# The last pass of a two-layer attention and MLP backward: row vectors prepared one set ahead on two partition pairs, and fourteen weight-gradient pieces moved into the first group

## The chip, the cores and the metric

The kernel runs on one core of a Trainium2 chip. The time is the device time of one execution in microseconds; three runs of the kernel before gave 1993.6, 1994.94 and 1997.81 us, median 1994.94 us. The engines are named as in the profile: PE is the matrix engine, PEld its weight loads, DVE, ACT and POOL are the vector, scalar and GpSimd engines, and SP only issues DMAs. DMAs that are issued from SP, ACT and POOL show up as the DMA queues q1, q10 and q0.

## The reference

One token goes through attention A, MLP B, A and B again with the same weights, and then back:

```
x = x + A(layernorm(x))      # layer 1:  q = x@wq, softmax(q k^T) v over 65536 cached keys, @wo
x = x + B(layernorm(x))      # layer 2:  relu(x@w1 + b1)^2 @ w2 + b2
x = x + A(layernorm(x))      # layer 3
x = x + B(layernorm(x))      # layer 4
grads = vjp(grad_out)        # of x, k_cache, v_cache, wq, wo, w1, b1, w2, b2
```

All data are bf16. `k_cache` and `v_cache` are 4 heads x 65536 x 128 (67 MB each), D is 1024, there are 32 query heads (8 to a cached head), F is 3584, `wq` is 1024 x 4096, `wo` 4096 x 1024, `w1` 1024 x 3584, `w2` 3584 x 1024. Each weight gradient is a sum of two outer products of vectors, one from each layer that uses the weight: for `w2`, for example, g4 gx^T + g2 dx2^T. So a weight gradient takes hardly any arithmetic, but each has to be written in full (7.3 to 8.4 MB).

## The kernel before, in words

The kernel goes over the cached keys and values four times: forward of layer 1, forward of layer 3, backward of layer 3, and a last pass (`attn_bwd4`) that does the backward of layer 1 and writes the gradients of the keys and values for both layers. The change is in this last pass, which starts at about 1217 us of the span.

The last pass takes the four cached heads ("groups") in the order 3, 2, 1, 0, and each group in 64 steps of 8 columns (8 x 128 keys). `pipeline` runs 256 + 7 iterations; in each it issues three stages, `vT` (8 transposes of V, L1015), `vS` two steps later (products with dO, L1035; every fourth step the tile X, whose halves come from DVE, L1042 and L1043, and from POOL, L1044 and L1045, and its transposes, L1050) and `k8` seven steps behind `vT` (dq, L1072; the gradients of 8 columns of K and V, L1082). The gradients leave PSUM by `evac` (L152 on ACT, L155 on DVE; whichever has less planned load) into one of three staging pairs, and after every fourth step POOL issues two stores of 1 MB (L1089, L1090). K and V come in slabs of 1 MB that SP issues (L278) into a ring of five areas as these come free; the second group's end adds two areas.

Beside the three stages an iteration can have background work, `bg[i]`, issued at its end and pinned behind what each engine has been given (`in_order`). There are two kinds. The first is the row dots: `og1.later` reads 8 rows of `wo` (256 KB each, 2 KB to a partition, L809) for each of the groups 2, 1 and 0, and `qg1.early` and `qg1.transposed` read rows of `wq` (L864); a row dot is a multiplication on DVE (L427) and a sum on ACT (L428). The second is the weight gradients, planned from iteration 73 (one after the end of the first group) to 244: 154 tasks, spread evenly. Of these 38 are pieces of `rows_into`: they turn four columns of two vectors into 512 elements in partitions 0 and 1 of `long_rows` or `short_rows` (two casts on DVE, L1103; four matmuls with two columns of weights, L1106; one evacuation of 2 x 512). The other 116 are units of `outer2`: two matmuls of 512 columns (L1133) with 128 partitions, all but two of them zero, an evacuation of 128 x 1024 (or less), and after every second unit a store of 512 KB (384 KB for some of `out_6`), issued by POOL (L1137). There is one set of rows at a time: the pieces for the next weight stand between the units of the one before and its own. The order is `out_8` (w2), `out_6` (w1), `out_4` (wq) for groups 3 and 2, `out_5` (wo), `out_4` for group 1. Group 0 of `out_4` follows behind the pipeline. The stores have five staging areas of 512 KB, four of them in the exponentials of the first group, which are free once this group is done.

`long_rows` is `area[12]` and `short_rows` a quarter of `area[13]`; both are set to zero by POOL (L1354, L1355). Of the eight `wo` rows of the second group, each has a buffer of its own, and SP issues them 30 iterations ahead.

Of the kernel before, what the change touches and what calls it, by code (L numbers as in the profile page):

```python
# [8 lines left out]
BF = mybir.dt.bfloat16  # L9
# [5 lines left out]
P = 128  # L15
# [3 lines left out]
def kernel(  # L19
# [52 lines left out]
    OG = 2048  # L72
# [1023 lines left out]

    def rows_into(rows, cols, nj):

        def piece(j0):
            jn = min(4, nj - j0)  # L1100
            cc = tmp.tile([P, 4, 2], BF, name="r2_cc")
            for l in range(2):
                nc.vector.tensor_copy(out=cc[:, 0:jn, l], in_=cols[l][:, j0:j0 + jn])  # L1103
            pt = ps_gg()
            for jj in range(jn):
                nc.tensor.matmul(pt[0:2, jj * P:(jj + 1) * P], lhsT=cc[:, jj, :], rhs=ident_b[:, :], start=True, stop=True)  # L1106
            evac(rows[0:2, j0 * P:(j0 + jn) * P], pt[0:2, 0:jn * P], kind="f32")
        for j0 in range(0, nj, 4):
            yield lambda j0=j0: piece(j0)

    def outer2(stages, out_dram, a_rows, K, b_rows, c0, N):
# [3 lines left out]
        av = a_rows[:, 0:K].rearrange("q (p k) -> q k p", k=KB)  # L1115
# [7 lines left out]
        for kb, per, n0, w in pieces:  # L1123
            for kk in range(per):
                for m0 in range(0, w, 1024):
                    def unit(kb=kb, per=per, n0=n0, w=w, kk=kk, m0=m0):
# [193 lines left out]
    ring.add(area[7], area[12])  # L1320
# [16 lines left out]
    ring.remove(area[7], area[12])  # L1337
# [4 lines left out]

    PS["pool"].release()
# [3 lines left out]
    long_rows, short_rows = area[12], part(area[13], 0, 1024)  # L1347
    wo_rows = Turn([part(area[13], i, 1024) for i in (1, 2)] + [part(area[5], 1, 1024)])
    e_first = [e_tiles[k][ORD4[0]] for k in (1, 3)]
# [3 lines left out]
    def rows_ready():  # L1353
        nc.gpsimd.memset(long_rows, 0.0)  # L1354
        nc.gpsimd.memset(short_rows, 0.0)  # L1355

    def gwq_tasks(gs, fresh=True):
        gs = sorted(gs)
        a, b = gs[0] * R, (gs[-1] + 1) * R
        if fresh:  # L1360
            yield from rows_into(short_rows, [L3["n"][:], L1["n"][:]], DC)
        yield from rows_into(long_rows, [dqT3[:, a:b], dqT1[:, a:b]], b - a)
        yield from outer2(stages, out_4, short_rows, D, long_rows, gs[0] * GD, len(gs) * GD)

    def gw_tasks():
        yield from rows_into(short_rows, [gx[:], dx2[:]], DC)
        yield from rows_into(long_rows, [L4["g"][:], L2["g"][:]], FC)
        yield from outer2(stages, out_8, long_rows, F, short_rows, 0, D)
        yield from rows_into(short_rows, [L4["n"][:], L2["n"][:]], DC)
        yield from rows_into(long_rows, [dh4[:], dh2[:]], FC)  # L1370
        yield from outer2(stages, out_6, short_rows, D, long_rows, 0, F)
        yield from gwq_tasks(ORD4[0:2])
        yield from rows_into(short_rows, [dx3[:], dx1[:]], DC)
        yield from rows_into(long_rows, [L3["oT"][:], L1["oT"][:]], HQ)
        yield from outer2(stages, out_5, long_rows, QD, short_rows, 0, D)
        yield from gwq_tasks(ORD4[2:3])
# [3 lines left out]
    first_rows = Turn(wo_rows.areas + [part(area[12], i, 1024) for i in range(4)])  # L1380
    og1.later(vbx1, ORD4[1], bg, 16, 5, first_rows, 30, nc.sync)
# [14 lines left out]
    def group_done(j):  # L1396
        if j == 1:
# [14 lines left out]
    for t in gwq_tasks(ORD4[-1:], False):  # L1412
        t()
# [32 lines left out]
```

## Time and profile before

| what | us |
|---|---|
| median of three runs | 1994.94 |
| profiled execution: device time | 1996.7 |
| profiled execution: span from first to last instruction | 1994.9 |
| busy PE, PEld, DVE, ACT, POOL | 1590.6, 1316.1, 1101.0, 1026.5, 204.4 |
| mean rate of the DMA engines over the span | 398 GB/s |
| mean granted clock of the matrix engine | 0.903 |

Times in the tables of stretches are microseconds from the start of the span. "DMA share" is the mean busy share of the core's 16 DMA engines; 1.0 means that all were busy all the time (overlapping packets let it read 1.01 or 1.02). A group of instructions is given with the idle time of its engine just before it and what ended that idle time. Idle time of an engine that is not the bottleneck costs nothing.

### The profile page before, as it was taken

To read this page: it belongs to the slowest core of one execution; us is meant where nothing else is said; L and a number is where in the kernel's file an instruction comes from. 1 tells how busy PE (TensorE), PEld (TensorE's weight loads), DVE (VectorE), ACT (ScalarE), POOL (GpSimd) and SP (SyncE) were. 2 spreads that over 40 slices of the span, in tenths; PEclk is the share of its full clock that TensorE was granted. 3 is DMA by queue.
4 is the path that set the end of the run, shared out by engine and by line. 5 is a ranking of instruction groups with operands and counts; after the bars stand their busy time and mean duration, and the time that the engine had idled before them with its cause. 6 is when DMAs were issued, how large, how long until landed. Compare 5 with 4: busy or idle time off the path is not lost.

```text
span 1994.9 us, 65729 instructions
## 1 busy us (share of the span) xinstructions
PE 1590.6 (80%) x29868; PEld 1316.1 (66%) x29924; DVE 1101.0 (55%) x1816; ACT 1026.5 (51%) x1284; POOL 204.4 (10%) x362
## 2 busy tenths in 40 slices
PE   7888886579888858888878876877888778788886
PEld 6878786578787757877777775555555545555464
DVE  4544431146444314645454456877677767787675
ACT  3543432034434314445444436876677667767775
POOL 0000000000000000000000001222122222212221
PEclk9998997669999976999889977999889978989898
DMA  9999999989999996999999996999999999999997
GB/s 395 426 423 421 411 408 410 406 317 419 425 421 420 425 409 275 397 418 412 412 412 396 403 390 240 412 425 424 387 418 408 423 406 367 423 372 420 423 422 302
DMA packets 119186, 793.86 MB, mean 398 GB/s; under 512 B 11756, under 2 KB 11770, under 8 KB 55290
## 3 DMA queue, kind: packets, MB, share of 16 engines
q1 hardware_dynamic: 82858, 604.02, 74.1%
q0 software_dynamic: 29136, 173.04, 21.0%
q10 hardware_dynamic: 6912, 12.59, 1.7%
q8 instruction: 234, 3.83, 0.8%
q14 instruction: 46, 0.38, 0.0%
HBM read 623.92 MB, written 165.69 MB: 396 GB/s over the span
## 4 chain that ended last, share of the span: by engine, by line
PE 38%; DMA 34%; DVE 10%; ACT 10%; issue 7%; another core or an unknown queue 0%; POOL 0%; SPq 0%; ACTq 0%; POOLq 0%; DVEq 0%
DMA pair<-in_A_v_cache_dram 15%; DMA pair<-in_A_k_cache_dram 8%; DMA out_dram<-pair 7%; PE ps_tr L667 6%; PE ps_sc L686 4%; PE ps_acc L729 4%; PE ps_gg L1082 4%; PE ps_tr L920 3%; PE ps_tr L1015 3%; ACT small L152 3%; ACT pair L152 3%; DVE pair L155 3%; DMA pair<-in_A_wo_dram 2%; DVE small L155 2%; PE ps_sc L941 2%
## 5 line engine op out<-in xcount | busy, mean ns | idle before, releaser
L155 DVE COPY small<-ps_tr 128x1024 bf16<-128x1024 bf16 x637 | 432.2, 688 | 338.1 <-PE ps_tr L667 172.8
L152 ACT COPY small<-ps_tr 128x1024 bf16<-128x1024 bf16 x371 | 372.8, 1015 | 387.6 <-PE ps_tr L667 206.8
L152 ACT CAST pair<-ps_gg 128x1024 bf16<-128x1024 f32 (+2 forms) x331 | 320.3, 983 | 141.1 <-PE ps_gg L1082 79.0
L155 DVE CAST pair<-ps_gg 128x1024 bf16<-128x1024 f32 x245 | 289.4, 1182 | 115.5 <-PE ps_gg L1082 91.3
L667 PE MATMUL ps_tr<-ident_b,pair 128*128 128x128 bf16 x3264 | 246.8, 225 | 29.2 <-DMA pair<-in_A_k_cache_dram 16.4
L1082 PE MATMUL ps_gg<-pair,small 64*128 64x512 bf16 x1024 | 201.5, 403 | 56.1 <-ACT pair L152 24.1
L667 PEld LDWEIGHTS <-pair 128*128 128x128 bf16 x3264 | 197.4, 101 | 34.8 <-DMA pair<-in_A_k_cache_dram 19.0
L729 PE MATMUL ps_acc<-eT,pair 128*128 128x64 bf16 x3840 | 170.4, 205 | 44.6 <-DMA pair<-in_A_v_cache_dram 39.8
L686 PE MATMUL ps_sc<-L_qpad,small 128*128 128x64 bf16 (+7 forms) x3456 | 173.9, 193 | 24.0 <-issue 10.7
L729 PEld LDWEIGHTS <-pair 128*128 128x128 bf16 x3840 | 154.0, 104 | 48.3 <-DMA pair<-in_A_v_cache_dram 42.9
L1015 PE MATMUL ps_tr<-ident_b,pair 128*128 128x128 bf16 x1792 | 163.4, 229 | 14.8 <-DMA pair<-in_A_v_cache_dram 11.6
L428 ACT ACTIVATE pair<-pair 128x1024 bf16<-128x1024 bf16 (+1 forms) x125 | 142.1, 1137 | 50.3 <-DVE pair L427 46.1
L920 PE MATMUL ps_tr<-ident_b,pair 128*128 128x128 bf16 x2048 | 155.6, 228 | 13.6 <-DMA pair<-in_A_v_cache_dram 9.8
L686 PEld LDWEIGHTS <-small 128*128 128x128 bf16 x3456 | 140.4, 99 | 34.6 <-ACT small L152 16.1
L1015 PEld LDWEIGHTS <-pair 128*128 128x128 bf16 x1792 | 115.7, 102 | 61.3 <-issue 42.8
L920 PEld LDWEIGHTS <-pair 128*128 128x128 bf16 x2048 | 128.6, 103 | 35.7 <-DMA pair<-in_A_v_cache_dram 17.8
L1082 PEld LDWEIGHTS <-small 64*128 64x128 bf16 x1024 | 60.5, 94 | 112.5 <-issue 85.0
L941 PE MATMUL ps_sc<-B_dOpad,small 128*128 128x64 bf16 (+7 forms) x2048 | 101.0, 193 | 16.0 <-ACT small L152 9.0
L1035 PE MATMUL ps_sc<-DOB,small 128*128 128x64 bf16 (+3 forms) x2048 | 112.1, 195 | 0.6 <-issue 0.2
L1035 PEld LDWEIGHTS <-small 128*128 128x128 bf16 x2048 | 87.0, 100 | 36.9 <-issue 32.0
L692 DVE TENSOR_REDUCE pm_all<-pair 128x8 f32<-128x512 f32 x64 | 43.9, 686 | 111.8 <-ACT pair L691 111.8
L941 PEld LDWEIGHTS <-small 128*128 128x128 bf16 x2048 | 80.1, 99 | 26.1 <-ACT small L152 14.1
(262 smaller groups left out, 1997.0 us busy)
## 6 DMA issues: line engine op xcount, KB each, us to landing
out_dram<-pair POOLq DMA_DIRECT2D x128, 1024.0 KB, 16.3
pair<-in_A_v_cache_dram SPq DMA_DIRECT2D x62, 2048.0 KB, 16.9
pair<-in_A_v_cache_dram SPq DMA_DIRECT2D x112, 1024.0 KB, 13.0
pair<-in_A_k_cache_dram SPq DMA_DIRECT2D x111, 1024.0 KB, 13.9
pair<-in_A_k_cache_dram SPq DMA_DIRECT2D x55, 2048.0 KB, 19.0
pair<-in_A_wo_dram SPq DMA_DIRECT2D x24, 1024.0 KB, 19.4
out_dram<-eT POOLq DMA_DIRECT2D x44, 512.0 KB, 16.5
pair<-in_B_w_dram SPq DMA_DIRECT2D x24, 896.0 KB, 15.1
```

The lines of the kernel that those rows point to most:

```text
L152: nc.scalar.copy(out=out, in_=in_)
L155: nc.vector.tensor_copy(out=out, in_=in_)
L428: nc.scalar.activation(out=view, in_=view, func=ACTF.Copy, accum_out=ycol)
L667: nc.tensor.transpose(pt[:, i, :], kb8[:, i, :], ident_b[:, :])
L686: nc.tensor.matmul(ps_s[:, slot:slot + w, :].rearrange("p a b -> p (a b)"), lhsT=kt[:, i, :], rhs=L["qpad"][:, g, 0:w, :].rearrange("p a b ...
L692: nc.vector.tensor_reduce(out=pm_all[:, :, c0 // UB], in_=S_sb[:, :, c0:c0 + un], axis=AX.X, op=ALU.max)
L729: nc.tensor.matmul(ps_o[:, :, :].rearrange("p a b -> p (a b)"), lhsT=vb8[:, i, :], rhs=eT[g][:, :, c:c + 8], start=(c == 0), stop=(c == C ...
L920: nc.tensor.transpose(pt[:, i, :], vb8[:, i, :], ident_b[:, :])
L941: nc.tensor.matmul(ps_dp[:, slot:slot + w, :].rearrange("p a b -> p (a b)"), lhsT=vt[:, i, :], rhs=dOpad[:, g, 0:w, :].rearrange("p a b -> ...
L1015: nc.tensor.transpose(pt[:, i, :], vb8[:, i, :], ident_b[:, :])
L1035: nc.tensor.matmul(ps_dp[:, slot:slot + w, :].rearrange("p a b -> p (a b)"), lhsT=vt[:, i, :], rhs=DOB[:, g, 0:w, :].rearrange("p a b -> p ...
L1082: nc.tensor.matmul(pg[:, t2 * 512:(t2 + 1) * 512], lhsT=xt[64 * t2:64 * t2 + 64, blk0 + half, :], rhs=GG[64 * t2:64 * t2 + 64, :, :, :].re ...
```

## The change

Rows are now made by `rows_moved`: the columns of both vectors are laid side by side (two casts), transposed once on PE, copied by DVE to `flat`, and two DMAs issued by POOL put the `nj` pieces of 256 bytes of each vector behind each other into one partition. A set of rows lies in partitions 0 and 1, or in 64 and 65; `outer2` takes the 64 partitions from `at_row` on, so one set can be made while the other is in use. `rows_into` is left for the last group only.

The first 14 units (of 28) of `out_8` move into the first group, two in an iteration, at iterations 3, 11, ... 51; until the first group is done there is a single staging area for them. The other 102 tasks are spread from iteration 73 to 244. The order of the weights becomes `out_8`, `out_6`, `out_5`, `out_4`.

`long_rows` is set to zero before the slabs of `w1` are read, so the ring borrows `area[13]` in place of `area[12]` there; `short_rows` is set to zero, and the first set of rows made, just before the last pass. The eight `wo` rows of the second group are now issued by ACT, 8 iterations ahead, into the three buffers of `wo_rows`.

```
+    def rows_moved(rows, cols, nj, flat=None):
+        cc = tmp.tile([P, 64], BF, name="rm_cc")
+        for l in range(2):
+            nc.vector.tensor_copy(out=cc[:, l * nj:(l + 1) * nj], in_=cols[l])
+        pt = ps_tr()
+        nc.tensor.transpose(pt[0:2 * nj, 0, :], cc[:, 0:2 * nj], ident_b[:, :])
+        if flat is None:
+            flat = tmp.tile([64, P], BF, name="rm_flat")
+        nc.vector.tensor_copy(out=flat[0:2 * nj, :], in_=pt[0:2 * nj, 0, :])
+        for l in range(2):
+            nc.gpsimd.dma_start(out=rows[l:l + 1, 0:nj * P], in_=flat[l * nj:(l + 1) * nj, :])
...
-    def outer2(stages, out_dram, a_rows, K, b_rows, c0, N):
+    def outer2(stages, out_dram, a_rows, K, b_rows, c0, N, at_row):
...
-        av = a_rows[:, 0:K].rearrange("q (p k) -> q k p", k=KB)
+        rows = slice(at_row, at_row + 64)
+        av = a_rows[rows, 0:K].rearrange("q (p k) -> q k p", k=KB)
...
-                                             rhs=b_rows[:, n0 + m0 + q0:n0 + m0 + q0 + qq], start=True, stop=True)
+                                             rhs=b_rows[rows, n0 + m0 + q0:n0 + m0 + q0 + qq], start=True, stop=True, tile_position=(at_row, 0))
...
-    ring.add(area[7], area[12])
+    long_rows, short_rows = area[12], part(area[13], 0, 1024)
+    nc.gpsimd.memset(long_rows, 0.0)
+    ring.add(area[7], area[13])
...
+    nc.gpsimd.memset(short_rows, 0.0)
+
+    def rows_a():
+        rows_moved(short_rows[64:66, :], [gx[:], dx2[:]], DC, area[13][0:64, 1024:1024 + P])
+        rows_moved(long_rows[64:66, :], [L4["g"][:], L2["g"][:]], FC, area[13][0:64, 1024 + P:1024 + 2 * P])
...
+    rows_a()
...
-    stages = Turn([part(e, i, OG) for i in range(2) for e in e_first] + [area[5][:, SLOT - OG:SLOT]])
+    stages = Turn([area[5][:, SLOT - OG:SLOT]])
...
-    first_rows = Turn(wo_rows.areas + [part(area[12], i, 1024) for i in range(4)])
-    og1.later(vbx1, ORD4[1], bg, 16, 5, first_rows, 30, nc.sync)
+    og1.later(vbx1, ORD4[1], bg, 14, 5, wo_rows, 8, nc.scalar)
...
-    at(bg, done[0], rows_ready)
-    i0, i1 = done[0] + 1, IPG * G - 12
-    tasks = list(gw_tasks())
-    for t, fn in enumerate(tasks):
-        at(bg, i0 + t * (i1 - i0) // len(tasks), fn)
+    tasks = list(outer2(stages, out_8, long_rows, F, short_rows, 0, D, 64))
+    na = len(tasks)
+    tasks += list(outer2(stages, out_6, short_rows, D, long_rows, 0, F, 0))
+    nb_ = len(tasks)
+    tasks += list(outer2(stages, out_5, long_rows, QD, short_rows, 0, D, 64))
+    tasks += outer_q(ORD4[0:2], 0) + outer_q(ORD4[2:3], 2 * GD)
+    n0, i0, i1 = 14, done[0] + 1, IPG * G - 12
+    place = [3 + 8 * (t // 2) for t in range(n0)] + [i0 + t * (i1 - i0) // (len(tasks) - n0) for t in range(len(tasks) - n0)]
+    for i, fn in zip(place, tasks):
+        at(bg, i, fn)
+    at(bg, 20, rows_b)
+    at(bg, place[na - 1] + 1, rows_c)
+    at(bg, place[nb_ - 1] + 1, rows_d)
+    at(bg, max(place[nb_ - 1], done[1]) + 2, lambda: rows_q(ORD4[0:2], 0))
+    at(bg, done[2] + 2, lambda: rows_q(ORD4[2:3], 2 * GD))
...
     def group_done(j):
-        if j == 1:
+        if j == 0:
+            stages.areas += [part(e_tiles[k][ORD4[0]], i, OG) for i in range(2) for k in (1, 3)]
+        elif j == 1:
             ring.add(e_area(1, ORD4[1]), e_area(3, ORD4[1]))
```

More of the change, by code (lines that the diff above doesn't have):

```diff
@@ L1336 @@
     og1.first(ORD4[0], dx1, vbx1)
-    ring.remove(area[7], area[12])
+    ring.remove(area[7], area[13])
     gb2 = add_cols(gx[:], dx2[:], "gb2")
@@ L1341, with rows_b, rows_c, rows_d @@
     col_to_dram(gb1, F, out_7, nc.gpsimd)
+    nc.gpsimd.memset(short_rows, 0.0)
+    def rows_a():
+        rows_moved(short_rows[64:66, :], [gx[:], dx2[:]], DC, area[13][0:64, 1024:1024 + P])
+        rows_moved(long_rows[64:66, :], [L4["g"][:], L2["g"][:]], FC, area[13][0:64, 1024 + P:1024 + 2 * P])
+    def rows_b():
+        rows_moved(short_rows[0:2, :], [L4["n"][:], L2["n"][:]], DC)
+        rows_moved(long_rows[0:2, :], [dh4[:], dh2[:]], FC)
+    def rows_c():
+        rows_moved(short_rows[64:66, :], [dx3[:], dx1[:]], DC)
+        rows_moved(long_rows[64:66, :], [L3["oT"][:], L1["oT"][:]], HQ)
+    def rows_d():
+        rows_moved(short_rows[0:2, :], [L3["n"][:], L1["n"][:]], DC)
+    def rows_q(gs, at_):
+        sl = slice(min(gs) * R, (max(gs) + 1) * R)
+        rows_moved(long_rows[0:2, at_:], [dqT3[:, sl], dqT1[:, sl]], len(gs) * R)
+    def outer_q(gs, at_):
+        return list(outer2(stages, out_4, short_rows, D, long_rows[:, at_:], min(gs) * GD, len(gs) * GD, 0))
+    rows_a()
     PS["pool"].release()
@@ L1345 @@
     load["act"] = load["dve"] = 0.0
-    long_rows, short_rows = area[12], part(area[13], 0, 1024)
     wo_rows = Turn([part(area[13], i, 1024) for i in (1, 2)] + [part(area[5], 1, 1024)])
-    e_first = [e_tiles[k][ORD4[0]] for k in (1, 3)]
-    stages = Turn([part(e, i, OG) for i in range(2) for e in e_first] + [area[5][:, SLOT - OG:SLOT]])
+    stages = Turn([area[5][:, SLOT - OG:SLOT]])
     dqT1 = vec.tile([P, HQ], F32, name="B1_dqT")
[L1353 to L1376, printed above, removed]
     bg = {}
     LAG4 = 7
-    first_rows = Turn(wo_rows.areas + [part(area[12], i, 1024) for i in range(4)])
-    og1.later(vbx1, ORD4[1], bg, 16, 5, first_rows, 30, nc.sync)
+    og1.later(vbx1, ORD4[1], bg, 14, 5, wo_rows, 8, nc.scalar)
     og1.later(vbx1, ORD4[2], bg, IPG + 14, 4, wo_rows, 8, nc.scalar)
@@ L1385 @@
     done = [IPG * (j + 1) + LAG4 + 1 for j in range(G)]
-    at(bg, done[0], rows_ready)
-    i0, i1 = done[0] + 1, IPG * G - 12
-    tasks = list(gw_tasks())
-    for t, fn in enumerate(tasks):
-        at(bg, i0 + t * (i1 - i0) // len(tasks), fn)
+    tasks = list(outer2(stages, out_8, long_rows, F, short_rows, 0, D, 64))
[13 more added lines that the diff above has]
+    at(bg, done[2] + 2, lambda: rows_q(ORD4[2:3], 2 * GD))
+    assert place[-R] > done[2] + 10 and place[-3 * R] > done[1] + 10
     qg1.early(ORD4[0:1], bg, done[1] + 16, 2.75, vbx1, wo_rows, 5)
@@ L1410 @@
     attn_bwd4(L1, L3, og1, og3, ORD4, eT1, eT3, dqT1, bg, group_done, streams)
-    for t in gwq_tasks(ORD4[-1:], False):
+    g = ORD4[-1]
+    for t in rows_into(long_rows, [dqT3[:, g * R:(g + 1) * R], dqT1[:, g * R:(g + 1) * R]], R):
+        t()
+    for t in outer_q([g], 0):
         t()
```

## The prediction

> **What bounds the kernel now.** I read the page's slices first, then a table of stretches of the last pass, then the groups that the change removes. The rate of the DMA engines by slices of 49.9 us:
>
> ```profile
> GB/s 395 426 423 421 411 408 410 406 317 419 425 421 420 425 409 275 397 418 412 412 412 396 403 390 240 412 425 424 387 418 408 423 406 367 423 372 420 423 422 302
> ```
>
> The last pass begins at 1217 us, in the slice with 240. The stretches of it (us, busy time of each engine, granted clock, DMA share, GB/s):
>
> ```profile
> core 0: us, PE busy (x) PEld busy (x) DVE busy (x) ACT busy (x) POOL busy (x), PEclk, DMA share, GB/s
> ...
> 1219.00:1237.00 18.00, 15.37 (x259) 11.77 (x259) 12.09 (x20) 11.45 (x13) 2.05 (x4) 0.96 0.10 41
> 1237.00:1250.00 13.00, 10.87 (x173) 7.25 (x169) 10.97 (x15) 10.73 (x13) 3.74 (x7) 1.00 0.82 307
> 1250.00:1377.00 127.00, 104.44 (x1608) 72.16 (x1609) 97.89 (x136) 95.54 (x107) 30.35 (x52) 0.99 1.01 421
> ...
> 1415.00:1450.00 35.00, 28.30 (x316) 17.25 (x319) 24.05 (x29) 23.33 (x27) 8.34 (x15) 0.84 0.97 365
> ...
> 1500.00:1525.00 25.00, 22.83 (x276) 14.21 (x278) 19.30 (x36) 19.23 (x21) 7.92 (x14) 1.00 1.00 393
> ...
> 1625.00:1700.00 75.00, 61.81 (x738) 39.17 (x744) 54.55 (x86) 51.87 (x65) 15.94 (x27) 0.83 0.97 375
> 1700.00:1750.00 50.00, 35.26 (x430) 22.44 (x434) 37.12 (x46) 33.32 (x40) 11.76 (x21) 0.89 1.02 422
> 1750.00:1800.00 50.00, 42.69 (x568) 27.30 (x569) 40.35 (x75) 37.11 (x47) 10.23 (x19) 0.94 0.96 373
> ...
> 1959.00:1995.00 36.00, 21.67 (x255) 12.43 (x256) 19.25 (x31) 17.39 (x18) 6.58 (x11) 0.82 0.64 256
> ```
>
> The reader should see that the DMA engines are the bound of this pass: from 1250 on they run at a share of 1.01 and 421 to 424 GB/s, whether the engines are 60 or 80% busy. The change leaves the bytes of the pass as they are. So it can gain only where the DMA engines fall short of 422 GB/s: a start gap (nearly idle for 18 us, 307 GB/s for 13 more), four dips, and the tail. The dips are worth 35 x (1 - 365/422) = 4.7, 25 x (1 - 393/422) = 1.7, 75 x (1 - 375/422) = 8.4 and 50 x (1 - 373/422) = 5.8: together 20.6 us. In the start gap the matrix engine sets the pace (15.37 of 18 us busy): five slabs are loaded, all areas are full, and the first store leaves at 1236.
>
> What the removed pieces do, by their matmul line:
>
> ```profile
> L1106 PE MATMUL ps_gg<-ident_b,r_cc x160: 216/218/311, 1386.0 to 1978.9; 128*2 128x128 bf16 x160
> ...
>   DVE r_cc L1103: 15.1, 27
> ...
>   ACT pair L152: 19.4, 18
>   DVE pair L155: 4.4, 5
> ```
>
> PE sat 15.1 us waiting for their casts, and ACT 19.4 us, DVE 4.4, for their matmuls: short serial chains in engines that work in order. They stand at 1386 to 1413, 1521 to 1542, 1673 to 1692, 1757 to 1790 and 1895 to 1908.
>
> **The change part by part.** The profiled execution took 1996.7 us (span 1994.9), 1.8 above the median of 1994.94. The sum is made against 1996.7 and its difference carried to the median.
>
> *Pieces of `rows_into` (38 of 40 go).* Busy time that goes: 152 matmuls x 0.22 = 33 us (pipelined, so about 15 of PE's own), 76 casts x 0.163 = 12 us of DVE, 38 evacuations x 0.7 = 27 us over ACT and DVE, and the waits above. Where the DMA engines are saturated this is worth nothing; they are the cover. It counts in the dips. Bounds: nothing, if the dips belong to the row dots (up to 1643.4 PE waited 3.1 us at once for DVE's vector work behind the last row dot of a group, where no piece stands); 20.6 us, if all dips go. I take the dips next to sets of pieces: 4.7 (1415 to 1450, just behind the first set), 19 x (1 - 385/422) = 1.7 (the set at 1673) and 33 x (1 - 378/422) = 3.4 (the set at 1757): **-9.8 us**. The dips at 1500 and 1637 to 1662 begin ahead of a set, and I leave them.
>
> *What replaces them:* nine `rows_moved`: nine transposes (0.23 each), 18 casts (0.16), nine copies (the nearest row, a cast of 28x128 out of PSUM, took 0.28) and 18 DMAs of 2 to 8 KB, each 0.52 us of POOL's time to issue: 9.4 us on an engine that is 24% busy there. POOL works in order: behind a row DMA that waits for its copy stand X's halves (L1044) and the stores (L1089). Cover: saturated DMA. Were that gone, each set would cost its chain once, about 2 us. Landing: 5.7 us (the small bias stores at 1152 to 1183) at best, 22.9 (the second 1 MB store at 1379) at worst; all sets but the first are made over 20 iterations ahead. On the DMA engines: the three bias stores, 44 runs of 256 bytes, are in a stretch (1150 to 1186) where their whole queue took 0.1% of 36 us, so 18 such DMAs take under 1 us: **+0.5 us** (0 to 1).
>
> The Trainium skill's "DMA: Bandwidth & Descriptors", section "Measured (HBM→SBUF, 128 partitions, SWDGE, issued from GpSimd)", speaks against these DMAs: under 64 KB a transfer is dominated by its descriptors, with 0.68 us of DMA time at 4 KB. By that 18 would cost 12.2 us in place of 0.5, and the sum below would be a gain of 1.5 in place of one of 6.6 - or a loss, if the dips stay.
>
> *First set (`rows_a`).* Its two copies stand between the last columns of `og1.first` on DVE, on the chain that opens the pass: 2 x 0.28; with the transposes +0.6 (0 to 1.5). POOL issues its four DMAs behind the first halves of X (1213.7 to 1215.4), so about 1217.5; landing 5.7 to 7.5 us later (the `wo` rows issued at 1205 took 7.1 to 7.8), so about 1224. PE reaches the first units, behind the X transposes of 1224.7, at about that time. I take no wait; 10 us at most.
>
> *Units in the first group.* Two units are 4 matmuls (0.38 each, overlapping: about 1.0 us of PE) and two evacuations (0.99 on ACT, 1.19 on DVE). In the gap PE is the pace, so one pair delays the first K and V stores by about 1.0 us (0 to 2). The first store (524 KB, 1.2 us at 422 GB/s) falls into the gap, the second (iteration 11, at about 1238) into the 307 GB/s stretch: -2.5. The other five run in a saturated stretch and make the first group 6.2 us longer, and the later groups, which lose seven, 8.7 shorter: the 2.5 again, not counted twice. Staging: one area; see the second rival.
>
> *The `wo` rows.* SP issued seven of the eight before the gap:
>
> ```profile
> 1205.40 4.64 SPq L809 DMA_DIRECT2D pair<-in_A_wo_dram  x7
> 1212.53 0.33 SPq L278 DMA_DIRECT2D pair<-in_A_k_cache_dram  x1
> 1215.56 0.33 SPq L278 DMA_DIRECT2D pair<-in_A_v_cache_dram  x1
> 1243.48 0.33 SPq L278 DMA_DIRECT2D pair<-in_A_k_cache_dram  x1
> ```
>
> From 1200 to 1222 the engines ran at 361 GB/s, so a row costs 262 KB / 361 = 0.73 us. Seven leave the stretch before the gap, where nothing waits for them; the slabs behind them on SP come 5 us earlier, and the gap opens earlier. Two (iterations 6 and 11) fall into the gap, five into saturated time: **+3.6 us**. ACT's issues (0.33 each) and landing (9.5 median against a lead of 8 x 2.3 = 18 us) are covered.
>
> *Other edits, at nothing:* the memsets (3.53 us at 1379 under a DMA share of 1.01; now at 1180, when POOL is idle); the ring's area 13 for 12 (one slab of `w1` may start up to 0.9 us later; the engines have a queue then); 64 partitions in place of 128 (a 64x512 matmul reads 403 ns, a 128x512 one 424; only the columns count); `out_5` ahead of `out_4`; fewer tasks in an iteration up to the end, where the DMA engines are saturated until 1959. The tail (36 us, 14 of them idle DMA) keeps its two pieces and eight units.
>
> Sum: -9.8 + 0.5 + 0.6 + 1.0 - 2.5 + 3.6 = **-6.6 us**: 1996.7 becomes 1990.1, and the median 1994.94 becomes **1988.3**.
>
> **The rivals.**
>
> *Hidden.* The dips are made by the row dots and by the ring of five slabs, and only move. For it: the dip at 1637 to 1662 has no piece near it, and DMA-bound stretches hold most of the pieces. Against: ACT's waits for L1106. Sum without the -9.8: +3.2, **1998**, within 0.2%.
>
> *Slower: the single staging area.* A unit's evacuation has to wait until the store of eight iterations before has landed.
>
> ```profile
> out_dram<-pair POOLq DMA_DIRECT2D x26, 1024.0 KB, 16.6
> ```
>
> That is 1250 to 1370; the second store of a pair took 18 to 22.9 us from 1263 on. A unit's store stands right behind such a pair, so 22.9 + 1.2 + about 1 until its issue = 25 us against 8 x 2.36 = 19 us: up to 6 us in which ACT or DVE, and soon PE, stand still, six times. Saturated DMA covers it while more than 6 us of transfers (2.5 MB) are queued; the staging pairs hold two stores of 2 MB, which speaks for the cover. It decides when the queue runs dry for 2 us each time: 12 - 6.6 = +5.4, **2000**; if dry for 3.5 each, 2009.
>
> *All dips go*, because 1.0 task in an iteration becomes 0.6: -20.6 + 3.2 = -17.4, **1977.5**. Against: the row dots stay.
>
> *The small DMAs cost their descriptors*, 0.68 us each on all engines: 12.2 for 0.5 gives +5.1, **2000**. The page named above is its ground; the 0.1% of the queue at 1150 to 1186 speaks against it.
>
> **How the numbers follow.** Runs of this kernel lie within 0.2% (4 us) of their median, so 0.2% is what can be told from no change: 1991 to 1999. Forecast 0.50 (0.45 of it below 1991; its own range 1984 to 1992), hidden 0.15, staging area 0.20, all dips 0.10, small DMAs 0.05. Faster 0.45 + 0.10 = 0.55, within 0.2% 0.05 + 0.15 = 0.20, slower 0.25. The range runs from 1976, where all dips go, to 2003, which takes in the staging rival up to 2.5 us dry each time.
>
> **What would show it.** The first group (to 1377 before) ends 8 to 12 us later, and groups two to four are 15 to 19 us shorter. The DMA share reads 1.01 through the first group still; if it drops there, with evacuations of L1147 waiting for a store, the staging area decides. The rate at the dips behind the old sets rises to above 400 GB/s; if it stays at 365 to 385, they belonged to the row dots. The wait of ACT for L1106 is gone but for the tail. If PE waits over 3 us for POOL's row DMAs at iteration 3, the first set is late. I am wrong above all if the dips come back in new places, since a DMA-bound pass gives nothing for freed engines.

## The result and the profile after

The changed kernel took 2000.47 us (median of 14 runs, 1996.11 to 2003.71), the kernel before 1995.1 in as many runs beside it: a ratio of 1.0027, 95% interval 1.002 to 1.0035. It is 5.4 us slower; the prediction had it 6.6 us faster. The profiled execution of the changed kernel took 2003.27 us (span 2001.5).

The rate of the DMA engines by slices of 50.0 us, from the page of the changed kernel:

```profile
GB/s 394 425 423 421 410 410 410 404 309 423 425 420 420 425 404 275 407 418 411 411 409 391 400 382 195 391 424 423 423 411 408 423 421 356 422 423 422 417 412 265
```

The slice that opens the last pass has 195 for 240, the one behind it 391 for 412, and the last one 265 for 302: the loss is at the two ends of the pass. The table of stretches of the changed kernel (us, busy time of each engine, granted clock, DMA share, GB/s):

```profile
core 0: us, PE busy (x) PEld busy (x) DVE busy (x) ACT busy (x) POOL busy (x), PEclk, DMA share, GB/s
1190.00:1219.00 29.00, 12.79 (x214) 11.31 (x213) 22.01 (x53) 20.72 (x27) 4.04 (x7) 0.72 0.90 353
1219.00:1237.00 18.00, 16.12 (x170) 12.53 (x168) 9.85 (x22) 6.99 (x7) 1.82 (x4) 0.60 0.29 101
1237.00:1250.00 13.00, 11.60 (x161) 7.08 (x157) 9.63 (x13) 9.62 (x10) 3.36 (x6) 1.00 0.37 138
1250.00:1377.00 127.00, 104.91 (x1487) 69.95 (x1488) 95.66 (x133) 93.33 (x105) 32.24 (x57) 0.96 1.00 411
...
1415.00:1450.00 35.00, 29.30 (x388) 18.89 (x387) 26.25 (x32) 25.36 (x30) 9.57 (x17) 0.98 1.02 422
1500.00:1525.00 25.00, 22.28 (x301) 15.06 (x298) 19.60 (x32) 17.11 (x19) 7.15 (x13) 0.94 0.99 387
1625.00:1700.00 75.00, 62.78 (x724) 38.43 (x725) 54.59 (x79) 51.60 (x64) 16.80 (x30) 0.83 0.95 378
1750.00:1800.00 50.00, 43.70 (x559) 27.47 (x558) 42.12 (x56) 38.69 (x47) 11.72 (x21) 0.94 1.02 422
1966.00:2001.50 35.50, 24.29 (x231) 11.20 (x227) 18.98 (x30) 16.15 (x17) 7.27 (x12) 0.66 0.60 241
```

The middle went much as forecast. Two of the dips that the prediction closed are closed (365 to 422 GB/s at 1415, 373 to 422 at 1750), and the two that it left are still there (387 at 1500, 378 at 1625 to 1700). These windows do not hold the same work, as the changed kernel is some 20 us later there; counted by the steps of `k8`, the picture is the same in both traces of each kernel: by the measure below, the loss between steps 176 and 192 goes (4.6 and 4.8 us, then none and 1.3), and so does that between 72 and 88, while the one between 144 and 152 stays (5.3 and 4.9 us, then 6.0 and 3.8). Groups two to four (to step 240) took 547.6 us for 565.7, within the 15 to 19 that were forecast (548.2 for 563.1 in the second traces, just under them). The first group ended at 1397.5, 20 us later (14.7 in a second trace) and not 8 to 12. In the gap the second row is richer (101 GB/s for 41), as the unit stores fall into it, but the third has 138 for 307, and before the gap, from 1190 to 1219, the rate is 353, where the kernel before has

```profile
1190.00:1219.00 29.00, 12.73 (x182) 11.24 (x182) 20.96 (x55) 19.55 (x26) 2.32 (x4) 0.61 1.01 388
```

To compare whole traces I use one measure, **lost DMA time**: the length of a stretch, less what its packets need at the median duration of their size in the trace (0.31 us for 8 KB, 0.16 for 4 KB, 0.084 for 2 KB, over 16 engines). Two executions of each kernel, the second from before_again and after_again below:

| kernel | 1190 to 1377 | 1377 to 1570 | 1570 to 1800 | 1800 to 1950 | 1950 to the end | span |
|---|---|---|---|---|---|---|
| before | 21.8, 22.3 | 5.4, 3.6 | 12.2, 12.2 | -1.3, -1.5 | 14.0, 14.1 | 1994.9, 1995.3 |
| after | 29.5, 26.6 | 1.9, 3.1 | 5.5, 4.1 | 0.4, 1.4 | 18.5, 17.4 | 2001.5, 1997.6 |

By the means the middle (1377 to 1950) lost 8.2 us for 15.3, so 7.1 were gained; the start lost 6.0 more, the tail 3.9 more, and the packets from 1190 on needed 1.65 more (most of it for bytes that had not been moved by 1190, where the count begins; two executions of one kernel differ by as much). The sum is +4.45, the difference of the mean spans (1999.55 and 1995.1).

### The profile page after: what moved, and what is told of

Same layout as the page of the kernel before. It is cut to its first block, busy times and chain, and to the rows that moved or that the text cites. A ratio compares the mean times of both kernels' runs of the same rounds, so it can differ in the third digit from the quotient of the medians.

```text
span 2001.5 us, 65442 instructions
## 1 busy us (share of the span) xinstructions
PE 1617.0 (81%) x29781; PEld 1314.0 (66%) x29781; DVE 1094.2 (55%) x1747; ACT 1023.8 (51%) x1266; POOL 212.2 (11%) x380
## 4 chain that ended last, share of the span: by engine, by line
PE 37%; DMA 37%; DVE 11%; ACT 8%; issue 5%; POOL 0%; SPq 0%; ACTq 0%; POOLq 0%; DVEq 0%
DMA out_dram<-pair 12%; DMA pair<-in_A_v_cache_dram 12%; DMA pair<-in_A_k_cache_dram 10%; PE ps_tr L667 6%; PE ps_sc L686 4%; PE ps_gg L1082 3%; PE ps_tr L920 3%; PE ps_acc L729 3%; PE ps_tr L1015 3%; DVE pair L155 3%; ACT pair L152 2%; ACT small L152 2%; PE ps_gg L1147 2%; DVE small L155 2%; PE ps_sc L941 2%
## 5 line engine op out<-in xcount | busy, mean ns | idle before, releaser
L155 DVE COPY small<-ps_tr 128x1024 bf16<-128x1024 bf16 x624 | 422.4, 688 | 338.4 <-PE ps_tr L667 173.8
L152 ACT COPY small<-ps_tr 128x1024 bf16<-128x1024 bf16 x384 | 385.3, 1014 | 413.7 <-PE ps_tr L667 208.1
L152 ACT CAST pair<-ps_gg 128x1024 bf16<-128x1024 f32 (+1 forms) x307 | 307.4, 1014 | 139.8 <-PE ps_gg L1082 84.6
L155 DVE CAST pair<-ps_gg 128x1024 bf16<-128x1024 f32 x243 | 295.4, 1218 | 142.4 <-PE ps_gg L1082 94.0
L1082 PE MATMUL ps_gg<-pair,small 64*128 64x512 bf16 x1024 | 214.2, 414 | 51.7 <-ACT pair L152 23.3
L667 PEld LDWEIGHTS <-pair 128*128 128x128 bf16 x3264 | 196.9, 101 | 35.7 <-DMA pair<-in_A_k_cache_dram 26.8
L1015 PE MATMUL ps_tr<-ident_b,pair 128*128 128x128 bf16 x1792 | 170.2, 236 | 1.7 <-ACT small L152 0.6
L1015 PEld LDWEIGHTS <-pair 128*128 128x128 bf16 x1792 | 119.1, 105 | 67.3 <-issue 66.5
L686 PEld LDWEIGHTS <-small 128*128 128x128 bf16 x3456 | 139.0, 99 | 32.6 <-ACT small L152 15.1
L1082 PEld LDWEIGHTS <-small 64*128 64x128 bf16 x1024 | 59.0, 94 | 96.0 <-issue 68.3
L1035 PEld LDWEIGHTS <-small 128*128 128x128 bf16 x2048 | 90.4, 102 | 43.8 <-issue 42.7
L1035 PE MATMUL ps_sc<-DOB,small 128*128 128x64 bf16 (+3 forms) x2048 | 118.3, 198 | 0.8 <-ACT small L152 0.8
L1147 PE MATMUL ps_gg<-pair 64*128 64x512 bf16 x240 | 83.1, 430 | 27.7 <-ACT pair L152 18.0
## 6 DMA issues: line engine op xcount, KB each, us to landing
out_dram<-pair POOLq DMA_DIRECT2D x128, 1024.0 KB, 18.5
pair<-in_B_w_dram SPq DMA_DIRECT2D x24, 896.0 KB, 14.7
```

The costliest lines, as they stand in the source:

```text
L152: nc.scalar.copy(out=out, in_=in_)
L155: nc.vector.tensor_copy(out=out, in_=in_)
L667: nc.tensor.transpose(pt[:, i, :], kb8[:, i, :], ident_b[:, :])
L686: nc.tensor.matmul(ps_s[:, slot:slot + w, :].rearrange("p a b -> p (a b)"), lhsT=kt[:, i, :], rhs=L["qpad"][:, g, 0:w, :].rearrange("p a b ...
L1015: nc.tensor.transpose(pt[:, i, :], vb8[:, i, :], ident_b[:, :])
L1035: nc.tensor.matmul(ps_dp[:, slot:slot + w, :].rearrange("p a b -> p (a b)"), lhsT=vt[:, i, :], rhs=DOB[:, g, 0:w, :].rearrange("p a b -> p ...
```

## The experiments

Ratios are to runs of the kernel before on the same chip, with their 95% interval. In the diffs, done[0] is iteration 72, the first behind the first group's last sums. Places of units and rows are iterations of `pipeline`; losses and times are counted by the steps of `k8`, which run seven iterations behind.

**The same kernels once more** (before_again, after_again: no edit).

> The kernel before once more, for a second trace. If the four dips between 1377 and 1950 belong to the pieces of rows_into, they stand at the same iterations and are worth 15 to 20 us again. If they come from where the queues happen to be, they stand elsewhere or are worth half.

> The changed kernel once more, for a second trace. Start theory: DMA time lost up to 1377 is 6 to 9 us more than in the kernel before again. Tail theory: the time from the last K and V load to the end is again some 50 us against 43.

One execution each: 1997.04 and 1999.35. Their traces are the second numbers above. From the landing of the last K or V load to the end they took 43.6 and 49.3 us (43.1 and 50.3 in the first traces), as the tail theory has it; the start lost 4.3 us more than before, less than the 6 to 9 of the start theory. The long dips of the kernel before, from 1570 to 1800, lost 12.2 us both times; the one at 1415 ran at 402 GB/s in the second trace, not 365, so 4.7 us was one execution's figure. Of the start's loss in the changed kernel some 3 us were one execution's too: there the matrix clock stood at half for 16.5 us between 1217 and 1245, in the second for 6.8, as in the second trace of the kernel before.

**The moved rows alone, late** (rows_only): the start of the pass as before, no units in the first group.

```
+    at(bg, done[0], rows_ready)      # the two memsets
+    at(bg, done[0], rows_a)
+    n0, i0, i1 = 0, done[0] + 2, IPG * G - 12
...
+    at(bg, done[0] + 2, rows_b)
```

> The rows by transposes and DMAs, one set ahead, alone: the first group, the wo rows, the memsets and the ring are those of the kernel before. Start theory (the changed kernel loses its time where the last pass opens, to the units and rows put there, and the dips really close): 1986 to 1989 us, 6 to 9 below before, k8 starts at 1227 as before and the rate from 1377 to 1950 stays above 415 GB/s. Tail theory (the later groups were sped up, but the end of the pass gives it back, whatever is done at its start): 1993 to 1999, all K and V loads done some 8 us earlier than 1951 and the time after that longer than 43 us by as much. Rows theory (the small DMAs and the stores they stand beside cost the time): 2000 or more.

Measured: 2007.13, ratio 1.0057 (1.0043 to 1.007). Three views of its trace: two stretches, the longest waits from 1385 to 1440, and the row DMAs (KB each, median us to landing):

```profile
1385.00:1400.00 15.00, 1.60 (x50) 1.49 (x48) 1.47 (x4) 1.37 (x2) 1.10 (x2) 0.65 1.02 423
1400.00:1425.00 25.00, 20.44 (x139) 10.75 (x139) 12.24 (x17) 11.50 (x13) 6.54 (x12) 0.53 0.56 211
```

```profile
ACT pair L152 <- PE ps_gg L1147: 18.8, 2, 16.9
...
PE ps_gg L1147 <- DMA pair<-rm_flat: 15.5, 1, 15.5
```

```profile
pair<-rm_flat POOLq DMA_DIRECT2D x4, 2.0 KB, 10.6
pair<-rm_flat POOLq DMA_DIRECT2D x4, 7.0 KB, 11.6
```

A 7 KB transfer stood behind 1 MB stores, and PE, which works in order, did 1.6 us of work in 15 while it waited. The DMA engines stayed busy for those 15 us with what was queued, and ran dry behind: 25 x (1 - 211/422) = 12.5 us lost. This is what a row DMA costs that is needed at once. In the changed kernel the same DMAs landed after 3.0 to 4.7 us at the empty start and after 14.4 to 14.9 us under full queues, and no wait of PE for them is in its trace:

```profile
pair<-pair POOLq DMA_DIRECT2D x2, 2.0 KB, 3.0
pair<-pair POOLq DMA_DIRECT2D x2, 7.0 KB, 4.7
pair<-rm_flat POOLq DMA_DIRECT2D x2, 2.0 KB, 14.4
pair<-rm_flat POOLq DMA_DIRECT2D x2, 7.0 KB, 14.9
```

**The moved rows alone, one set ahead** (rows_ahead, and once more as rows_ahead_2): the same with

```
+    at(bg, 54, rows_ready)
+    at(bg, 55, rows_a)
+    n0, i0, i1 = 0, done[0] + 1, IPG * G - 12
...
+    at(bg, 62, rows_b)
```

> Rows by transposes and DMAs alone, as in rows_only, but the first set made at iterations 54 and 55, so that its row DMAs have landed when the units begin at 73. The start is that of the kernel before. If the late first set (12 us without transfers at 1400 to 1425) was all that was wrong with rows_only: 1990 to 1995, and a gain on the kernel before if the dips of the later groups close with the pieces. If rows by DMA cost time of their own: 1998 or more.

> The moved rows alone once more, beside the two above, for a second trace and a comparison on the same chip: 1.0006 (0.9997 to 1.0016), with 27 to 28 us of half clock in the last 30 us, 4 to 9 us lost between 1570 and 1800 us, and 17 to 18 in the tail.

Measured: 1.0006 (0.9997 to 1.0016) and 1.0003 (0.9992 to 1.0013): the time of the kernel before. Lost DMA time, the two traces: 22.8 and 22.6 to 1377, 5.7 and 6.4, then 4.8 and 2.6 from 1570 to 1800 (12.2 before), 0.9 and 0.5, and 18.0 and 19.8 in the tail (14.0 before). So with the rows alone 8.5 us are gained there, and 4.9 of it come back in the tail, 2.1 and 1.5 between 1800 and 1950 and ahead of 1570. This is the step that the prediction didn't have, and it needs none of the change's edits at the start.

Where it comes back can be read behind the loads. The last K or V load landed at 1943.1 and 1942.7 us, against 1951.8 and 1951.6 in the kernel before, 8.7 and 8.9 us earlier; from there to the end it took 50.3 and 52.6 us against 43.1 and 43.6. The stretch from this landing to the last matmul of the iterations' sums (L1072), in the kernel before, the changed kernel and rows_ahead:

```profile
1951.80:1970.20 18.40, 14.80 (x239) 9.96 (x237) 12.58 (x16) 13.14 (x14) 3.33 (x6) 1.00 0.78 319
```

```profile
1951.20:1974.20 23.00, 21.83 (x308) 14.55 (x306) 16.52 (x20) 17.65 (x19) 4.54 (x8) 0.87 0.75 305
```

```profile
1943.10:1965.90 22.80, 21.18 (x308) 14.02 (x308) 16.33 (x21) 16.80 (x18) 4.53 (x8) 0.93 0.72 293
```

Against the engines' work the loads are done earlier: 14 steps of `k8` are left behind them in place of 12, and PE is busy for 93 to 95% of this stretch in place of 80% (84% in rows_ahead_2). So the loads got ahead of the matrix engine, and what they gained became engine work behind them. This is read from both traces of each kernel; no run changed it by itself.

**No units in the first group** (no_first_units) and **no pairs at iterations 3 and 11** (pairs_from_19), both from the changed kernel:

```
-    n0, i0, i1 = 14, done[0] + 1, IPG * G - 12
+    n0, i0, i1 = 0, done[0] + 1, IPG * G - 12
```

```
+    n0, i0, i1 = 10, done[0] + 1, IPG * G - 12
-    place = [3 + 8 * (t // 2) for t in range(n0)] + ...
+    place = [19 + 8 * (t // 2) for t in range(n0)] + ...
```

> The changed kernel with all 116 units behind the first group; rows, memsets, ring and wo rows stay changed. Start theory with the units as its cause: 1988 to 1992, since only the wo rows (3.6 us) are left of what the start lost. Start theory with the wo rows as its cause: 1996 to 2000. Tail theory: 1998 to 2003, as the changed kernel.

> The changed kernel without the pairs of units at iterations 3 and 11; the pairs at 19 to 51 stay, the four units go behind the first group. Start theory with the units in the gap as cause: 3 to 6 us faster than the changed kernel, 1995 to 1997. If the single staging area of the first group is the cause: within 2 us of the changed kernel, 1999 to 2002. Tail theory: the same as the changed kernel.

Measured: 1.0016 (1.0004 to 1.0028) and 1.003 (1.0021 to 1.004). The first is 1998.1 us, where the theories of the `wo` rows and of the tail both have it; the second 2001.1, not the 1995 to 1997 that would have made the pairs in the gap the cause. Without units there the time is 2.2 us nearer to the kernel before (1.0027 against 1.0016; the intervals overlap, so that this price is not clear of the noise), with ten of them from iteration 19 on it is the changed kernel's. Both start alike: 26.3 us lost to 1377, 4.3 more than before and 0.3 to 3.2 less than the changed kernel. The pairs in the gap are thus not what the units cost; no one place holds the rest of their price.

**Units in the first group without the moved rows** (units_only): the kernel before with the first 14 units at 3, 11, ... 51, its rows by `rows_into`, the memsets, the ring and the `wo` rows as in the change.

```
+    nr = 2 + 7
+    for fn in tasks[:nr]:
+        fn()
+    for t, fn in enumerate(tasks[nr:nr + 14]):
+        at(bg, 3 + 8 * (t // 2), fn)
...
```

> The kernel before with fourteen units of the first weight gradient in the first group, rows by rows_into in one set on partitions 0 and 1 (the first set made before the pass), memsets, ring and wo rows as in the change. Start theory: slower than before by more than the change was, 2003 to 2008, since the start is lost and the dips stay. Tail theory: 1995 to 1999. Rows theory: 1990 to 1995, since no small DMA is left.

Measured: 1.0032 (1.002 to 1.0045). 32.7 us lost to 1377, the most of all, since nine pieces stand ahead of the first units. From 1570 to 1800 it lost 3.8 us although `rows_into` makes its rows. The set of ten pieces that stood in a dip in the kernel before (first row) stands in a saturated stretch here, with the same 40 matmuls of L1106 (second row):

```profile
1757.00:1790.00 33.00, 27.39 (x384) 17.54 (x381) 27.39 (x61) 23.98 (x32) 6.77 (x12) 0.95 0.97 378
```

```profile
1728.00:1768.00 40.00, 34.23 (x492) 22.91 (x492) 32.00 (x59) 30.88 (x41) 9.01 (x17) 0.96 1.02 422
```

So the pieces alone don't make that dip, and a kernel that keeps them loses as little there as one without.

**The `wo` rows alone** (wo_on_act): the kernel before with one line of the change.

```
-    og1.later(vbx1, ORD4[1], bg, 16, 5, first_rows, 30, nc.sync)
+    og1.later(vbx1, ORD4[1], bg, 14, 5, wo_rows, 8, nc.scalar)
```

> The kernel before with one edit: the eight wo rows of the second group issued by ACT, 8 iterations ahead, in three buffers. Start theory with the wo rows as its cause: 3 to 5 us slower than before, 1998 to 2000, the DMA engines idle before 1219 already and the first group longer by that. If they are hidden: within 1 us of before.

Measured: 1.001 (1.0001 to 1.0018), 2.0 us slower by this ratio (the medians differ by 0.9). (The eight rows share seven buffers in the kernel before, not eight, so the eighth is issued at 1250 there.) The stretches of its start:

```profile
1190.00:1219.00 29.00, 13.18 (x186) 11.31 (x187) 20.80 (x56) 19.41 (x26) 2.32 (x4) 0.68 0.89 342
1219.00:1237.00 18.00, 15.40 (x261) 12.10 (x259) 11.66 (x18) 10.98 (x13) 2.21 (x4) 0.95 0.08 19
1237.00:1250.00 13.00, 11.28 (x181) 7.76 (x178) 11.57 (x15) 10.60 (x13) 3.09 (x7) 1.00 0.89 338
```

The same fall from 388 to 342 GB/s ahead of the gap as in the changed kernel, and 24.8 us lost to 1377, 2.7 more than before: the `wo` rows are dearer behind the gap than ahead of it. From 1570 to 1800 this trace lost 7.1 us for 12.2 with the same code there, so part of those dips goes with small shifts of what comes before: the losses between steps 72 and 88, behind the first set of pieces, and between 144 and 152 are gone, with every piece in its place.

**The tail: half tiles and the clock.** In the changed kernel the last eight units run at half clock throughout; in the kernel before the clock comes back during them. Stretches of the kernel before and of the changed one:

```profile
1974.90:1981.70 6.80, 5.24 (x21) 2.33 (x20) 3.46 (x10) 3.61 (x4) 1.06 (x2) 0.50 0.59 234
1981.70:1985.00 3.30, 2.12 (x8) 1.07 (x8) 2.16 (x2) 2.02 (x2) 0.72 (x1) 1.00 0.98 400
```

```profile
1984.40:1988.00 3.60, 3.08 (x12) 1.36 (x12) 0.88 (x3) 2.26 (x3) 1.05 (x2) 0.50 0.54 219
1988.00:1991.40 3.40, 3.06 (x7) 0.92 (x6) 2.16 (x2) 1.31 (x2) 0.72 (x1) 0.50 1.03 424
1991.40:1995.00 3.60, 2.86 (x7) 0.75 (x5) 1.52 (x2) 2.02 (x2) 1.16 (x2) 0.50 0.86 328
```

PE is busy for 3.06 us of 3.4 there and still gets 0.50, over three windows. What differs is the tile (the part of the array that a matmul uses): 64 partitions of the array's rows in place of 128. The test gives `outer2` a count of units to be multiplied over all 128 partitions, with the other half of the rows zero; in after_ends128 these are the units of the last group and the first four, in ra_tail128 (rows_ahead with it) those of the last group.

```
...
+                        rows, av = (slice(0, 128), avs[1]) if all_ else (half, avs[0])
...
+    at(bg, place[n5 - 1] + 1, lambda: nc.gpsimd.memset(short_rows[64:128, :], 0.0))
...
+    for t in outer_q([g], 0, 99):
```

> The changed kernel with the units of the last group (eight, behind the last K/V store) and the first four units (iterations 3 and 11) multiplied over all 128 partitions, as the kernel before does; the other half of the rows is zero there (one memset of short_rows, rows 64 to 127, once out_5 is done). Theory, half tiles hold the clock down: in the traces of the changed kernel the eight units stand in 25.9 and 27.3 us of half clock and their 128-column-wide matmuls take 611 ns, against 423 in the kernel before, although PE is busy for 3.1 of each 3.4 to 3.6 us there. With 128 partitions the clock comes back during them as before: half clock in the last 30 us at most 17 us, the stretch from the end of the iterations to the end back from 27.6 to 25 us, the median about 2.5 us below the changed kernel's, at 1.0014 of the kernel before. Rival, the clock follows the gaps between matmuls, which are longer here for the store of a staging pair: half clock still over 24 us, 27 to 28 us to the end, 1.0027.

> The moved rows alone (one set ahead, no units in the first group, the start of the pass as in the kernel before) with the last group's eight units over 128 partitions. If half tiles hold the clock down, the stretch from the end of the iterations to the end goes from 27.6 to 25 us and the ratio from 1.0006 to 0.9993. If the clock follows the gaps, 27 to 28 us and 1.0006. Between iterations 240 and 248 ACT and DVE wait 4 us for a staging pair's store in either case.

Measured: 1.0014 (1.0004 to 1.0024) and 1.0001 (0.999 to 1.0012). Stretches of after_ends128, and the matmuls of the last units with their mean ns, of the kernel before, of the changed kernel and of after_ends128:

```profile
1984.50:1988.10 3.60, 3.27 (x7) 1.09 (x7) 1.23 (x1) 1.85 (x2) 0.39 (x2) 0.50 0.99 401
1988.10:1991.50 3.40, 1.80 (x7) 0.86 (x6) 2.45 (x2) 2.02 (x3) 1.14 (x2) 0.99 0.89 352
```

```profile
L1133 PE MATMUL ps_gg<-pair 128*128 128x512 bf16 x15 | 5.0, 423 | 2.7 <-DVE eT L155 1.3 <-ACT eT L152 0.7 <-DVE pair L155 0.7
```

```profile
L1147 PE MATMUL ps_gg<-pair 64*128 64x512 bf16 x16 | 8.0, 611 | 1.2 <-DVE eT L155 0.7 <-ACT eT L152 0.2
```

```profile
L1150 PE MATMUL ps_gg<-pair 128*128 128x512 bf16 x16 | 6.3, 496 | 2.0 <-DVE eT L155 1.6 <-ACT eT L152 0.2
```

With 128 partitions the clock came back during the units in all five traces of kernels with this edit, the three below among them (13.7 us at half clock, 17.1 in one, and then full), and in the four of kernels whose units have 128 partitions anyway (before, before_again, wo_on_act, units_only: 6.8 to 13.7 us), with 64 in none of the seven that have the moved rows and units of 64 (24.6 to 27.4 us at half clock to the end). So units of half tiles do keep the clock down. The size was smaller than expected: from the end of the iterations (the last L1072) to the end of the kernel 26.9 and 26.7 us for 27.5 to 27.8, where the kernel before has 24.9, not back to 25. The rival was wrong on the cause; of its numbers, the ratio 1.0027 is outside the interval, barely. In time the gain is not resolved: 1.0001 stands beside 1.0003 for rows_ahead_2 on the same chip, and 1.0014 has an interval that overlaps that of 1.0027. That 1.0014 was also the number expected is luck, since the 0.6 to 0.9 us of the tail don't make 2.5. The wait of 4 us for a staging pair's store that ra_tail128 was to have "in either case" was 1.3 and 1.8 us in its trace.

The other 2 us of that stretch are most likely in an order of instructions that is the same in every trace of a kernel: behind the last matmul of the iterations' sums (L1072) stand 14 matmuls of K's and V's gradients (L1082, about 0.5 us each) in the kernel before and 18 in the changed one, in both traces of each. Nothing in the diff names them; their last one ends 7.0 us behind the last L1072 before, and 10.1 to 10.5 after. Over all traces it ends 7.0 to 7.7 us behind it where 14 stand there (three traces), 8.4 and 10.1 where 16 do (no_first_units, ra_tail128_early), and 9.9 to 10.5 where 18 do (eleven, units_only among them, whose rows aren't moved and whose tiles are whole). So the time goes with the count and not with the moved rows; but no run changed this order by itself, so its price is argued, not shown.

**The units' end moved** (ra_tail128_early to iteration 232, ra_tail128_late and after_ends128_late to 254; 244 in all others):

```
-    n0, i0, i1 = 0, done[0] + 1, IPG * G - 12     # 14 for 0 in after_ends128_late
+    n0, i0, i1 = 0, done[0] + 1, IPG * G - 24     # early
+    n0, i0, i1 = 0, done[0] + 1, IPG * G - 2      # late
```

> The same with the units of groups two to four ending at iteration 232 in place of 244. Theory, the stores of the last units stand ahead of the last K and V stores, so ACT and DVE wait 4 us for a pair at about iteration 241 and the DMA engines are idle for it behind (3.6 us lost between iterations 240 and 244, against 1.3 in the kernel before): with the units out of the way the wait is under 1 us, 1.3 are lost there, and the end comes 2 us earlier, 0.9983. Rival, the loads run ahead instead and the compute behind them is what the end waits for: no change against the kernel beside it, or 1 us slower by denser units from iteration 73 on.

> The moved rows alone with the last eight units over 128 partitions, and the units of groups two to four ending at iteration 254 in place of 244 (232 made the wait for a staging pair's store at 1939 us 5.9 us long and the time 1.0017 of the kernel before, against 1.0001 with 244). Theory, the loss between iterations 240 and 248 comes from unit stores that stand ahead of the K and V stores, and is smaller the thinner they are spread: no wait over 2.5 us for a pair behind 1935 us, at most 3 us lost between iterations 240 and 248 (4.0 with 244, 5.6 with 232), and 1 to 2 us faster, 0.9993. Rival, the units of the last ten iterations now take the engines' time where nothing hides it, 8 x about 1 us behind the last loads: up to 5 us slower, 1.002, with the loss moved behind iteration 248.

> The changed kernel with the units at both ends over 128 partitions and the units ending at iteration 254 in place of 244. By the theory 1 to 2 us below its 1.0014: 1.0007, with less than 3.5 us lost between iterations 240 and 248 (5.1 before); by the rival 1.002 to 1.004 with the loss behind iteration 248. The start of the pass is untouched and stays 5 us longer than in the kernel before.

(The losses that these texts put between iterations 240 and 244, or 248, are those between steps 244 and 248, or 252, of `k8`.) Measured: early 1.0017 (1.0007 to 1.0028), late 1.0006 (0.9997 to 1.0016), late from the changed kernel 1.0013 (1.0003 to 1.0023). The wait in question, from the waits of the changed kernel between 1935 and 1965 us (us in total, times, longest):

```profile
ACT pair L152 <- DMA out_dram<-pair: 4.1, 1, 4.1
...
DVE pair L155 <- DMA out_dram<-pair: 3.8, 1, 3.8
```

Early was the wrong way: the units are denser, the wait grew to 5.9 us on the one engine and 6.4 on the other, and the time got longer. Late took the wait away (none over 2.5 us behind 1935 in either trace; 3.8 us lost between steps 244 and 252, for 4.0 and 5.1, though in ra_tail128_late 2.1 new ones stand just ahead, between 240 and 244), and the times didn't follow: 1.0006 for 1.0001, 1.0013 for 1.0014. So that wait is not what sets the end, and the theory behind these three runs falls; the rival of the early run, that the end waits for the compute behind the loads, fits the stretches shown with rows_ahead. No version beat the kernel before.

## Why the prediction was wrong

The step that failed is that a closed dip was booked as time off the end, with the tail put at nothing. rows_ahead shows it by itself: the dips close, and the time is 1.0003 to 1.0006 of the kernel before (1.0001 in ra_tail128, with whole tiles at the end). In the traces of the changed kernel the sum is off by 11.05 us (+4.45 for -6.6): 3.9 in the tail, 3.3 in the start, 2.7 in the dips and 1.15 in the packets.

**The dips, -9.8: near in size, the cause not shown.** 7.1 us were gained in the middle, at the places named; ACT's wait for L1106 is gone but for the tail. The 4.7 at 1415 was too much by one execution's luck. The reading that the dips at 1500 and 1637 to 1662 belong to something else than the pieces held. But that the pieces made the other dips isn't shown: in units_only ten of them stand in a saturated stretch, and in wo_on_act the dip behind the first set goes while they stay. (Of the 15.1 us that PE is said to have waited for their casts, 9.4 are waits of its weight loads, PEld, and 5.7 its own.) The rival *all dips go* is out. Of *hidden*, the causes (row dots, the ring of five slabs) were put to no test, but its "only move", at the time of the kernel before, is what rows_ahead measured; what the changed kernel lost beyond it is in the start.

**The tail at nothing: wrong, by 3.9 us.** The prediction costed the freed engines and the tail apart, with "The tail (36 us, 14 of them idle DMA) keeps its two pieces and eight units". The code of the tail did keep them. But its 14 us were not fixed: in rows_ahead, where the rows with their half tiles and the order of the weights are the only change, step 240 of `k8` starts 3 to 7 us earlier, the last load lands 9 us earlier, and the end stays, with two more steps of the engines' work left behind that load. Behind the last L1072 0.6 to 1.0 us are the clock under half tiles (the step "64 partitions in place of 128 ... only the columns count" looked at the duration of a warm matmul and not at the clock it runs by), the order of L1082 probably 2 us. How much of the 3.9 us each part has is open; taking away the one long wait between steps 244 and 252 changed nothing.

**The start, +2.7 forecast (0.6 + 1.0 - 2.5 + 3.6): 6.0 measured.** By its terms:

- *Seven `wo` rows, +3.6*: 2.7 us in the trace of wo_on_act and 2.0 in its timed ratio. Right in mechanism, a little large.
- *First set, +0.6 (0 to 1.5)*: no_first_units and pairs_from_19 lost 1.5 us more than wo_on_act, at the upper bound. The first store of K's gradients left 21.2 and 21.6 us behind the pass's first transpose of V (L1015) in these, 19.3 and 19.8 before, 19.8 with the `wo` rows alone. PE did not wait for the row DMAs.
- *Unit pairs, +1.0 and -2.5*: the term of the start with the wrong sign. Two pairs stand ahead of the second K and V stores, not one; the second K store left 32.0 us behind that transpose in after_again and 35.7 in the profiled execution, 29.7 and 30.1 without pairs: about 2 us for two pairs, where the clock was no worse than before. What the two 524 KB stores filled in the gap, the later K and V stores left empty. The net was +0.3 in the second trace and +3.2 in the first, where the clock was at half for longer, for the -1.5 in the sum (+0.4 and +0.1 in after_ends128 and after_ends128_late, which start alike but for the tile). In time it decides nothing: pairs_from_19, without these two pairs, is no faster. The first store did fall into the gap, as the row with 101 GB/s shows; but giving PE work in a gap that PE paces did not shorten it.

POOL's instructions in order of time (start, us, line, operation, the idle time before it), of the kernel before and then of the changed one, show it:

```profile
1236.16 0.55 POOL L1089 DMA_DIRECT2D out_dram<-pair  x1 [3.22 <-ACT pair L152]
...
1244.71 0.53 POOL L1089 DMA_DIRECT2D out_dram<-pair  x1 [3.58 <-ACT pair L152]
```

```profile
1232.90 0.56 POOL L1151 DMA_DIRECT2D out_dram<-pair  x1 [12.64 <-ACT pair L152]
...
1244.20 0.55 POOL L1089 DMA_DIRECT2D out_dram<-pair  x1 [4.48 <-ACT pair L152]
...
1248.04 0.53 POOL L1151 DMA_DIRECT2D out_dram<-pair  x1 [2.76 <-ACT pair L152]
...
1254.38 0.53 POOL L1089 DMA_DIRECT2D out_dram<-pair  x1 [3.73 <-ACT pair L152]
```

K's first store (L1089) left at 1236 before and at 1244 after, its second at 1245 and 1254, with a unit's store (L1151) ahead of each. Part of these 8 and 10 us is the clock of this execution: in the second traces they left at 1239 and 1241, and at 1247 and 1251.

**The small DMAs, +0.5: right.** The packets from 1190 on took 752.8 and 754.6 us before, 755.7 and 755.0 after: +1.65, within the 1.8 between two executions of one kernel. With the moved rows alone they took 751.2 and 753.4. The row DMAs' own packets can be counted in the traces: the changed kernel moves 112 more of 256 bytes, 88 more of 512 and 368 more of 4 bytes than the one before, and these took 0.5 us of the 16 engines together. So the 12.2 us of that rival are ruled out (and its first mention, "a gain of 1.5", doesn't follow: 12.2 for 0.5 makes the sum +5.1, as the prediction itself has it later). The figure for 4 KB in the Trainium skill's "DMA: Bandwidth & Descriptors", section "Measured (HBM→SBUF, 128 partitions, SWDGE, issued from GpSimd)", does not fit these transfers. What they cost here is their landing time.

**The single staging area.** Evacuations did wait up to 3.5 us for a store between 1250 and 1377, but the queue covered it: nothing was lost between 1300 and 1377 (-0.5 us). Its forecast of 2000, like that of the small DMAs, is the time that came; the mechanism of neither is, so that is luck.

By timed ratios the parts are `wo` rows 2.0 us, moved rows 0.6 to 1.2 and first-group units 2.2 (1.0027 less 1.0016), which leaves 0.0 to 0.6 of the 5.4 for the first set at the start. Each of these carries an uncertainty of about 2 us, so that they add up is no proof of any one of them.

## What to carry to other kernels

In a pass that transfers bound, closing dips may only move work earlier, as it did here: before it is booked as a gain, ask what the end waits for (how much of the engines' work is left when the last load has landed), and treat the tail's idle time as a term that changes with the rest and not as a constant. Look at the order of instructions behind the last loads in the built program, since four more matmuls stood there after an edit elsewhere. Work put into a start gap that an engine paces delayed the very stores that would end the gap; and a small transfer that was needed at once cost the wait for the queue that it stood behind (15.5 us), the same transfer a set ahead no wait at all.

## What the runs showed of the hardware

A matmul over 64 partitions didn't count as a full one for the granted clock in the tail. At a busy share of 0.79 to 0.90 over three windows the clock stayed at 0.50 under 64x512 matmuls, for the 9 us that they lasted; under 128x512 ones it returned to 1.0 between 2.2 and 7.1 us after the first of them, in the kernel before out of a stretch with a busy share of 0.77 (5.24 of 6.8 us). At half clock both kinds read some 580 to 650 ns, at full clock the 128-partition ones 377; in mean the units' matmuls read 611 ns with 64 partitions and 423 to 568 with 128. In the iterations, where 64x512 matmuls (L1082) come in pairs over both halves and between full ones, the clock stood at 1.00 in whole stretches (1500 to 1525 us in the kernel before), so this was seen for units of half tiles that stand alone. The Trainium skill's "TensorE: Matmul & The Clock Gate", section "What's actually happening", has the clock follow how busy the matrix engine has been, watched in windows of about 3.4 us; the traces agree in the steps (half-clock stretches of 3.4, 6.8, 10.2 and 13.7 us), but here the share of time busy was not enough to tell, and the part of the array in use was.
